# The last tile of a fused feed-forward kernel: each product evacuated from a PSUM tile of its own, the kept partial accumulated in PSUM, the last product in two column halves

## The chip, the cores and the metric

One core of a Trainium2 chip. The metric is the device time of one execution in microseconds (us).

Engines: PE does matmuls, DVE is VectorE, ACT is ScalarE, SP issues most transfers. PSUM is the memory that PE writes its results to. The kernel takes it in pieces of 512 FP32 values per partition, called banks here. To evacuate a result is to take it out of PSUM with another engine.

## The reference

```python
def reference(A_x, A_wqkv, A_wo, B_x, B_w_gate, B_w_up, B_w_down):
    xn = layernorm(A_x)                                  # 2048 x 1024, bf16
    s = linear_attention(xn, A_wqkv) @ A_wo              # 32 heads
    g = silu((silu(xn @ B_w_gate) * (xn @ B_w_up)) @ B_w_down)   # F = 3584
    return A_x + s * g
```

(Shortened: the linear attention is not touched by the change.)

## The kernel before

The down product `h @ w_down` is computed for a pass of 1024 tokens by 2x2 blocks, with seven block products in place of eight. A block here is 128 tokens by 512 output columns. A first phase leaves partial sums (`kept`: `s1` and the pair `s34`, FP32, in SBUF). A second phase adds three more products for each 128-token tile `t`, each a sum over `NFG` = 14 steps, each step one matmul: the pair `zw` and then `x_`. The last tile of the last pass is handled by `finish`, in which the products run one after the other so that the pair can be evacuated while the last product runs.

Shortened, with the pool lines simplified:

```python
CW = 512; NFG = 14; P = 128
pps = ctx.tile_pool(name="p3ps", bufs=4, space=PSUM)   # one bank each
ppd = ctx.tile_pool(name="p3pd", bufs=2, space=PSUM)   # two banks each
# ... (cut)
def fin(p, t, cc, y, eng1, eng2, out_eng, cols=None):  # y * s + x, then store
    # ... (cut: io holds x and s, loaded earlier)
    eng1.tensor_tensor(out=y[:, cs], in0=y[:, cs], in1=io[:, 1, cs], op=ALU.mult)
    eng2.tensor_tensor(out=io[:, 0, cs], in0=y[:, cs], in1=io[:, 0, cs], op=ALU.add)
    out_eng.dma_start(out=out2[...], in_=io[:, 0, cs])
# ... (cut)
def mm(out, lhs, rhs, first, lastk):
    nc.tensor.matmul(out, lhsT=lhs, rhs=rhs, start=first, stop=lastk, skip_group_check=True)

def finish(t):
    alloc(t, "b")
    x_, _, zw = bk[t]
    s1, s34 = kept[t]
    for q in (1, 2):
        for k in range(NFG):
            prods_b(t, k, True)[q]()           # into zw[:, 0, :], then zw[:, 1, :]
    d = m4.tile([P, 2, CW], FP32, name="dd", tag="m4")
    c11 = k2([P, CW], FP32, "c11")[:]
    g_ = k2([P, 2, CW], BF16, "g12")
    g11 = k2([P, CW], BF16, "g11")[:]
    nc.vector.tensor_tensor(out=d[:], in0=zw[:], in1=s34, op=ALU.add)
    nc.scalar.activation(out=g_[:], in_=d[:], func=ACT.Silu, scale=rch)
    fin(p, t + TPB, 0, g_[:, 0, :], *fin_e)
    fin(p, t, 1, g_[:, 1, :], *fin_e)
    for k in range(NFG):
        prods_b(t, k, True)[0]()               # into x_
    hs_ = [slice(i * CW // 2, (i + 1) * CW // 2) for i in range(2)]
    for cs in hs_:
        nc.vector.tensor_tensor(out=c11[:, cs], in0=x_[:, cs], in1=s1[:, cs], op=ALU.add)
        nc.scalar.activation(out=g11[:, cs], in_=c11[:, cs], func=ACT.Silu, scale=rch)
    for cs in hs_:
        fin(p, t, 0, g11, *fin_e, cols=cs)
```

In the listings of the profile, L882 and L883 are the two operations of `fin` (called output operations below), L910 is the matmul of `mm`, and L994, L995, L1002 and L1003 are the adds and Silus of `finish`.

## Time and profile before

| | before |
|---|---|
| time, first 3 runs | 767.11 us median (766.46 to 768.77) |
| span of the profiled run | 767.3 us |
| last matmul ends | 761.36 us |
| last VectorE instruction ends | 764.54 us |
| from there to the end of the span | 2.77 us |

From the page of the kernel before, first the span and the busy time of PE (us, share of the span, number of instructions), then the chain of work that ended last, as shares of the span by engine:

```profile
span 767.3 us, 10482 instructions
...
PE 754.1 (98%) x3717; PEld 349.6 (46%) x3717; DVE 551.5 (72%) x1076; ACT 345.8 (45%) x473; POOL 287.4 (37%) x413
...
PE 92%; DVE 4%; ACT 1%; DMA 1%; issue 1%; SPq 0%; ACTq 0%; DVEq 0%
```

PE is busy 98% and holds 92% of the chain. Work of other engines counts only where PE doesn't cover it, and at the end of the kernel that is everything after the last matmul. Timeline of PE at the end of the kernel before (start us, length us, engine, line, operation, number merged); the first line holds the last two matmuls of the tile before and the 28 of the pair:

```profile
751.70 6.64 PE L910 MATMUL dzw<-w_sb,hT 128*128 128x512 f16 x30
758.17 3.19 PE L910 MATMUL dx<-w_sb,hT 128*128 128x512 bf16 x14
```

Timeline of DVE, and below it of ACT, in the same stretch; brackets give the idle time before the instruction and what ended it:

```profile
757.05 0.43 DVE L883 TENSOR_TENSOR io<-g,io 128x512 bf16<-128x512 bf16 x1
758.38 1.23 DVE L994 TENSOR_TENSOR dd<-dzw,kept 128x1024 f32<-128x1024 f32 x1 [0.90 <-PE dzw L910]
760.82 0.42 DVE L882 TENSOR_TENSOR g<-g,io 128x512 bf16<-128x512 bf16 x1 [1.21 <-ACT g L995]
...
762.07 0.42 DVE L883 TENSOR_TENSOR io<-g,io 128x512 bf16<-128x512 bf16 x1
762.41 0.75 DVE L1002 TENSOR_TENSOR c<-dx,kept 128x256 f32<-128x256 f32 x2
763.40 0.29 DVE L882 TENSOR_TENSOR g<-g,io 128x256 bf16<-128x256 bf16 x1 [0.24 <-ACT g L1003]
...
764.25 0.29 DVE L883 TENSOR_TENSOR io<-g,io 128x256 bf16<-128x256 bf16 x1
```

```profile
759.63 1.15 ACT L995 ACTIVATE g<-dd,hsc 128x1024 bf16<-128x1024 f32 x1 [4.28 <-DVE dd L994]
762.86 0.91 ACT L1003 ACTIVATE g<-c,hsc 128x256 bf16<-128x256 f32 x2 [2.08 <-DVE c L1002]
```

Read them together. DVE waits 0.90 us for both products of the pair although the first was complete 3 us earlier, adds 1024 columns at once, and waits 1.21 us for one wide Silu. Its four output operations for the pair then run until 762.49. PE ended at 761.36, so the half adds of the last product (L1002) start 1.05 us late, held up by DVE's own order of work, not by PE. From the last matmul to the last DVE instruction it is 3.18 us.

### The profile page before, as it was taken

Reading aid. Unit: us, or ns where it says so; the run is one execution under the profiler, and the core shown is the slowest. Engines: PE = TensorE matmul, PEld = TensorE weight load, DVE = VectorE, ACT = ScalarE, POOL = GpSimd, SP = SyncE. Lnnn points to the kernel's source line nnn. Section 1 sums busy time; section 2 is a strip of 40 time slices with the busy share of each in tenths; the row PEclk is TensorE's granted clock in tenths of the full one; section 3 lists DMA queues with packets and bytes.
Section 4 is the critical chain, followed back from the end, with each engine's and each line's share of the span. In section 5 each row is a group of like instructions: output and inputs, shape, how many; then the busy total and the mean of one; then the engine's idle time right before and its main releaser. Section 6 shows DMA issues by size and latency. Waiting matters only on the chain.

```text
span 767.3 us, 10482 instructions
## 1 busy us (share of the span) xinstructions
PE 754.1 (98%) x3717; PEld 349.6 (46%) x3717; DVE 551.5 (72%) x1076; ACT 345.8 (45%) x473; POOL 287.4 (37%) x413
## 2 busy tenths in 40 slices
PE   7999999999999999999999999999999999999996
PEld 3544444444444444444444444444444444444443
DVE  6788557997666588878889885358676776787335
ACT  3545667788853566566447411132323223201111
POOL 0477499959685255858656000110000000200000
PEclk9999999999999999999999999999999999999999
DMA  9945868769889769898888227399654444530923
GB/s 308 352 95 114 229 221 274 248 222 259 237 304 262 256 228 312 283 333 298 308 309 290 89 81 262 113 356 334 229 185 167 165 169 175 187 114 23 296 73 117
DMA packets 105396, 170.29 MB, mean 222 GB/s; under 512 B 34688, under 2 KB 82176, under 8 KB 94720
## 3 DMA queue, kind: packets, MB, share of 16 engines
q1 hardware_dynamic: 94960, 121.00, 50.3%
q0 software_dynamic: 7936, 44.31, 15.0%
q10 hardware_dynamic: 2448, 4.33, 1.6%
q8 instruction: 29, 0.48, 0.3%
q14 instruction: 23, 0.19, 0.1%
HBM read 111.67 MB, written 50.59 MB: 211 GB/s over the span
## 4 chain that ended last, share of the span: by engine, by line
PE 92%; DVE 4%; ACT 1%; DMA 1%; issue 1%; SPq 0%; ACTq 0%; DVEq 0%
PE zw L725 25%; PE kv_ps L486 14%; PE dzw L910 13%; PE xb L725 12%; PE s_ps L659 7%; PE yb L725 6%; PE dx L910 6%; PE q_ps L170 4%; PE dy L910 3%; PE kvz L508 1%; DMA xp<-in_A_x_dram 1%; DVE o_blk L640 1%; PE nd_ps L632 1%; DVE pqT L141 1%; DVE pqT L153 0%
## 5 line engine op out<-in xcount | busy, mean ns | idle before, releaser
L725 PEld LDWEIGHTS <-w_sb 128*128 128x128 f16 (+1 forms) x1568 | 152.2, 98 | 184.3 <-issue 1.7
L725 PE MATMUL xb<-xnT,w_sb 128*128 128x512 bf16 x448 | 115.0, 379 | 1.1 <-ACT sg L800 1.1
L486 PE MATMUL kv_ps<-wkv_sb,xnT 128*128 128x512 bf16 x512 | 115.5, 383 | 0.4 <-DVE xnT L473 0.2
L725 PE MATMUL zw<-xnT,w_sb 128*128 128x512 bf16 x448 | 105.8, 379 | 0.0
L725 PE MATMUL zw<-S,w_sb 128*128 128x512 f16 x448 | 105.8, 379 | 0.0
L280 POOL TENSOR_TENSOR w_sb<-w_sb 128x512 f16<-128x512 bf16 x42 | 48.9, 1165 | 96.7 <-DVE w_sb L268 36.3
L247 ACT ACTIVATE w_sb<-w_sb 128x2048 bf16<-128x2048 bf16 x42 | 79.9, 1902 | 9.1 <-DMA w_sb<-in_B_w_up_dram 7.1
L910 PE MATMUL dx<-w_sb,hT 128*128 128x512 bf16 x224 | 82.8, 379 | 0.0
L486 PEld LDWEIGHTS <-xnT 128*128 128x128 bf16 x512 | 49.0, 98 | 57.2 <-issue 2.4
L910 PEld LDWEIGHTS <-hT 128*128 128x128 bf16 (+1 forms) x448 | 43.8, 98 | 52.9
L910 PE MATMUL dzw<-w_sb,hT 128*128 128x512 f16 (+1 forms) x224 | 64.4, 379 | 0.0
L170 PE MATMUL q_ps<-xnT,wq_sb 128*128 128x512 bf16 x256 | 58.2, 379 | 0.0
L753 DVE SCALAR_TENSOR_TENSOR s<-yb,rc_all,s 128x512 f32<-128x512 f32 x42 | 31.5, 749 | 37.0 <-ACT s L752 37.0
L659 PE MATMUL s_ps<-wo_sb,oT 128*128 128x512 bf16 x256 | 57.8, 379 | 0.0
L725 PE MATMUL yb<-S,w_sb 128*128 128x512 f16 x224 | 57.4, 379 | 0.0
L801 ACT ACTIVATE sg<-cg 128x1024 bf16<-128x1024 f32 x28 | 29.6, 1057 | 56.6 <-DVE cg L794 56.6
L794 DVE SCALAR_TENSOR_TENSOR cg<-zw,rc_all,s 128x1024 f32<-128x1024 f32 x28 | 35.9, 1283 | 25.4 <-PE zw L725 14.0
L850 POOL TENSOR_TENSOR hs<-hT 128x512 f16<-128x512 bf16 x2 | 2.5, 1258 | 132.6 <-ACT sg L801 132.6
L281 POOL TENSOR_TENSOR w_sb<-w_sb 128x512 f16<-128x512 bf16 x42 | 50.1, 1193 | 3.3
L283 POOL TENSOR_TENSOR w_sb<-w_sb 128x512 f16<-128x512 bf16 x42 | 50.8, 1210 | 0.0
L282 POOL TENSOR_TENSOR w_sb<-w_sb 128x512 f16<-128x512 bf16 x42 | 49.8, 1186 | 0.0
L884 POOL DMA_DIRECT2D out_dram<-io x16 | 8.7, 542 | 101.9 <-DVE io L883 101.6
(148 smaller groups left out, 1099.3 us busy)
## 6 DMA issues: line engine op xcount, KB each, us to landing
w_sb<-pk_g SPq DMA_DIRECT2D x27, 1024.0 KB, 6.0
pk_g<-w_sb POOLq DMA_DIRECT2D x14, 1024.0 KB, 5.4
pk_u<-w_sb POOLq DMA_DIRECT2D x14, 1024.0 KB, 6.4
w_sb<-wd SPq DMA_DIRECT2D x14, 1024.0 KB, 5.0
w_sb<-pk_u SPq DMA_DIRECT2D x14, 1024.0 KB, 4.9
w_sb<-wd SPq DMA_DIRECT2D x14, 768.0 KB, 5.8
w_sb<-in_B_w_gate_dram SPq DMA_DIRECT2D x14, 512.0 KB, 5.3
w_sb<-in_B_w_down_dram SPq DMA_DIRECT2D x28, 256.0 KB, 4.5
```

The source lines that it names most:

```text
L170: nc.tensor.matmul(q_ps[:], lhsT=wq_sb[:, dc, g * P:(g + 1) * P], rhs=xn_ap(dc, btok), start=(dc == 0), stop=(dc == DC - 1))
L247: nc.scalar.activation(out=junk, in_=raw_view(key, t), func=ACT.Square, accum_out=asum[:])
L280: nc.gpsimd.tensor_tensor(out=T1, in0=b12, in1=b11, op=ALU.subtract)
L281: nc.gpsimd.tensor_tensor(out=T2, in0=b22, in1=T1, op=ALU.subtract)
L282: nc.gpsimd.tensor_tensor(out=T3, in0=b22, in1=b12, op=ALU.subtract)
L283: nc.gpsimd.tensor_tensor(out=T4, in0=b21, in1=T2, op=ALU.subtract)
L486: mm = nc.tensor.matmul(kv_ps[:], lhsT=xn_ap(dc, tok), rhs=wkv_sb[:, dc, c * CW:(c + 1) * CW], start=(dc == 0), stop=(dc == DC - 1))
L659: mm = nc.tensor.matmul(s_ps[:], lhsT=oT[:, c, ttok], rhs=wo_sb[:, c, cc * CW:(cc + 1) * CW], start=(c == 0), stop=(c == G - 1))
L725: mm = nc.tensor.matmul(out, lhsT=lhs(k), rhs=rhs(k), start=(first and k == 0), stop=(k == HK - 1), skip_group_check=True)
L753: nc.vector.scalar_tensor_tensor(out=s2[:], in0=y_[:], scalar=rc, in1=s1[:], op0=ALU.mult, op1=ALU.add)
L794: nc.vector.scalar_tensor_tensor(out=d12, in0=zw[:], scalar=rc, in1=s2[:, None, :].to_broadcast([P, 2, TB]), op0=ALU.mult, op1=ALU.add)
L910: nc.tensor.matmul(out, lhsT=lhs, rhs=rhs, start=first, stop=lastk, skip_group_check=True)
```

## The change

The intent: let the two products of the pair be evacuated one by one, so that DVE is free when the last product ends; take the last add off DVE by copying `s1` into PSUM beforehand and accumulating on it; and finish one column half of the last product while PE computes the other.

"Own banks" stands for the first of these: a PSUM tile, an add and a Silu for each product of the pair. The name misleads in one point: the two products lay in different banks before too, `zw[:, 0, :]` and `zw[:, 1, :]` of a tile of two. What is new is that each is added and passed through Silu by itself.

The whole diff:

```diff
             def finish(t):
-                alloc(t, "b")
-                x_, _, zw = bk[t]
+                ps = [ppd.tile([P, 2, CW], FP32, name="dz", tag="d")[:, 0, :]]
+                ps += [pps.tile([P, CW], FP32, name="df%d" % i, tag="s")[:] for i in range(3)]
                 s1, s34 = kept[t]
-                for q in (1, 2):
+                t1, t2 = slice(t * P, (t + 1) * P), slice(TB + t * P, TB + (t + 1) * P)
+                hs_ = [slice(i * CW // 2, (i + 1) * CW // 2) for i in range(2)]
+                for i in range(2):
+                    nc.scalar.copy(out=ps[2 + i][:, 0:CW // 2], in_=s1[:, hs_[i]])
+                for q, (r0, cc) in enumerate(((t + TPB, 0), (t, 1))):
                     for k in range(NFG):
-                        prods_b(t, k, True)[q]()
-                d = m4.tile([P, 2, CW], FP32, name="dd", tag="m4")
-                c11 = k2([P, CW], FP32, "c11")[:]
-                g_ = k2([P, 2, CW], BF16, "g12")
+                        lhs = h[:, 2 * k, t2].bitcast(F16) if q else h[:, 2 * k + 1, t2]
+                        mm(ps[q], lhs, wb(k, 2 - q), k == 0, k == NFG - 1)
+                    d = k2([P, CW], FP32, "d%d" % q)[:]
+                    g_ = k2([P, CW], BF16, "g%d" % q)[:]
+                    nc.vector.tensor_tensor(out=d, in0=ps[q], in1=s34[:, q, :], op=ALU.add)
+                    nc.scalar.activation(out=g_, in_=d, func=ACT.Silu, scale=rch)
+                    if q == 0:
+                        f0 = (r0, cc, g_)
+                fin(p, *f0, *fin_e)
+                fin(p, r0, cc, g_, *fin_e)
                 g11 = k2([P, CW], BF16, "g11")[:]
-                nc.vector.tensor_tensor(out=d[:], in0=zw[:], in1=s34, op=ALU.add)
-                nc.scalar.activation(out=g_[:], in_=d[:], func=ACT.Silu, scale=rch)
-                fin(p, t + TPB, 0, g_[:, 0, :], *fin_e)
-                fin(p, t, 1, g_[:, 1, :], *fin_e)
-                for k in range(NFG):
-                    prods_b(t, k, True)[0]()
-                hs_ = [slice(i * CW // 2, (i + 1) * CW // 2) for i in range(2)]
-                for cs in hs_:
-                    nc.vector.tensor_tensor(out=c11[:, cs], in0=x_[:, cs], in1=s1[:, cs], op=ALU.add)
-                    nc.scalar.activation(out=g11[:, cs], in_=c11[:, cs], func=ACT.Silu, scale=rch)
-                for cs in hs_:
+                for i, cs in enumerate(hs_):
+                    o_ = ps[2 + i][:, 0:CW // 2]
+                    for k in range(NFG):
+                        mm(o_, h[:, 2 * k + 1, t1], wb(k, 0)[:, cs], False, k == NFG - 1)
+                    nc.scalar.activation(out=g11[:, cs], in_=o_, func=ACT.Silu, scale=rch)
                     fin(p, t, 0, g11, *fin_e, cols=cs)
```

## The prediction

> **What bounds the kernel.** TensorE. The page gives PE 98% of the 767.3 us span at 0.9+ granted clock, and the chain of waits is 92% PE. The change touches only `finish`, which handles the last token tile of the last down stage, so it can pay only where PE no longer covers the other engines: after the last matmul. The timeline of the end shows:
>
> - PE runs the three products of `finish` from about 752.1 us: 28 matmuls of the two-bank pair to 758.34, then 14 of the last product to 761.36 (pitch 0.216 us for 512 columns).
> - DVE, in order: outputs of the tile before until 757.48; idle 0.90 until the pair ends; the 1024-wide add 758.38–759.61 (1.23 us); idle 1.21 for the ScalarE Silu (1.15 us); four output operations 760.82–762.49. Only then, 1.05 us after PE ended, come the two half adds (762.41–763.2), Silu (0.5 us each), four half-wide output operations, last end 764.54.
> - From there to the end of span 2.76 us: the output DMA (1.6 us from issue to landing) and the closing drains.
>
> So 3.2 us lie between the last matmul and the last DVE instruction; the chain of waits there goes through the wide add, wide Silu, and DVE.
>
> **What the change does.** PE's columns are unchanged (14+14 half matmuls instead of 14 full ones in the last product: 14 more matmuls and weight loads). A half matmul has 256 columns; the groups with 129–132 columns run at about 80 ns each (10.1–10.3 us busy for 128), 512 columns at 216 ns, so I estimate 0.108–0.115 us for 256, weight load hidden. The Trainium skill, "TensorE: Matmul & The Clock Gate", section "Back-to-back issue gap", gives N/2.4+2.5 ns, 109 ns; the trace agrees at 512. So PE should end within 0.1 us of 761.36.
>
> Removed: the 1024-wide add and Silu, both half adds. Added: two 512-wide adds (0.68 each), two 512-wide Silus (0.71), two 256-wide ScalarE copies into PSUM (under 0.45 us each, estimate from 0.585 for 512), at about 755.4–756.2, long before the last product starts.
>
> Estimated new order: first add 757.5–758.2 (in the former 0.90 us gap; its product is complete at 755.3); second add 758.38–759.06; its Silu to 759.8; four output operations 759.1–760.9; first half complete at about 759.85, Silu to 760.3, two DVE operations to 761.5; second half complete 761.4, Silu to 761.9, two DVE operations to 762.5, DMA.
>
> The last DVE end moves from 764.54 to about 762.5: 2.0 us less, all on the critical path: 1.05 us of DVE queueing, 0.4 of half add, and one half's output work overlapped. The DMA tail should stay near 2.76.
>
> Accumulating on the copied data rests on the has_written bits left set by earlier full-bank products ("PSUM — Partial Sum Buffer", "The four PSUM rules": engine writes leave the bits alone, the matmul adds where they are set). No run here shows it yet; it costs no time.
>
> **Prediction:** 767.11 − 2.0 = 765.1 us, range 763.8 to 766.8. Chances: faster by over 2% 0.003, within 2% 0.99, slower 0.007.
>
> **What would show it.** Right: 28 matmuls of 256 columns in the last 3.1 us of PE; no DVE idle wait for the pair before the first add; DVE free when the second half ends; about 1.1 us from last matmul to last DVE end (3.2 before). Wrong: half matmuls at 0.13 us or more; PE waiting for the copies or for a bank; the output operations of the first two products still running at 761.4.
>
> **What would make it wrong.** A 256-column pitch set by the weight load (up to +1 us), a longer DMA tail, or run spread: the three runs before span 2.3 us, larger than the gain.

## The result, and the profile after

| | before | after |
|---|---|---|
| time, 4 runs each | 767.8 us median (766.46 to 768.77) | 764.17 us median (763.73 to 764.54) |
| ratio | | 0.9954 (95%: 0.9935 to 0.9972) |
| span of the profiled run | 767.3 | 762.5 |
| first matmul of `finish` starts | 752.13 | 749.32 |
| last matmul ends | 761.36 | 758.58 |
| last matmul end to last VectorE end | 3.18 | 1.16 |
| from there to the end of the span | 2.77 | 2.75 |

A ratio here is the mean time of one kernel's runs over that of the other's of the same rounds, so it isn't quite the ratio of the medians. Executions over 1.5% slower than the fastest of the same kernel are left out of the means. (752.13 is worked out: 28 matmuls, 0.216 us apart, ahead of the end of the pair.)

The measured 764.17 us lies within the range, but the difference of the medians, 3.6 us, is larger than the 2.0 predicted. The page of the changed kernel, the same three lines:

```profile
span 762.5 us, 10513 instructions
...
PE 752.3 (99%) x3731; PEld 350.5 (46%) x3731; DVE 551.0 (72%) x1075; ACT 346.6 (45%) x476; POOL 287.7 (38%) x413
...
PE 90%; DVE 5%; DMA 2%; POOL 1%; issue 1%; ACT 1%; SPq 0%; ACTq 0%; DVEq 0%
```

(The chain's larger share of DVE isn't the tail: over the first 30 us it runs mostly through DVE and POOL after the change, and through PE before.)

Timelines of the changed kernel's end: PE, then DVE, then ACT.

```profile
749.32 3.19 PE L910 MATMUL dz<-w_sb,hT 128*128 128x512 f16 x14
752.34 6.24 PE L910 MATMUL df<-w_sb,hT 128*128 128x512 bf16 x42
```

```profile
754.35 0.68 DVE L997 TENSOR_TENSOR d<-dz,kept 128x512 f32<-128x512 f32 x1
755.56 0.69 DVE L997 TENSOR_TENSOR d<-df,kept 128x512 f32<-128x512 f32 x1 [0.53 <-PE df L910]
756.17 0.41 DVE L882 TENSOR_TENSOR g<-g,io 128x512 bf16<-128x512 bf16 x1
...
757.56 0.42 DVE L883 TENSOR_TENSOR io<-g,io 128x512 bf16<-128x512 bf16 x1
757.90 0.28 DVE L882 TENSOR_TENSOR g<-g,io 128x256 bf16<-128x256 bf16 x1
...
759.12 0.29 DVE L882 TENSOR_TENSOR g<-g,io 128x256 bf16<-128x256 bf16 x1 [0.61 <-ACT g L1008]
759.45 0.29 DVE L883 TENSOR_TENSOR io<-g,io 128x256 bf16<-128x256 bf16 x1
```

```profile
752.44 0.66 ACT L990 COPY df<-kept 128x256 f32<-128x256 f32 x2
...
758.62 0.47 ACT L1008 ACTIVATE g<-df,hsc 128x256 bf16<-128x256 f32 x1 [1.06 <-PE df L910]
```

The two adds are apart, DVE has finished the pair and the first half when the last half comes, and it waits 0.61 us for ACT. After the last matmul only one Silu of 256 columns and two half-wide output operations are left: 1.16 us. The copies into PSUM were done 2.3 us before the last product's first matmul. PE is not slower: from the first matmul of `finish` to the last end it took 9.26 us (758.58 − 749.32), against 9.23 (761.36 − 752.13).

So 2.0 us of the 4.8 us between the two spans lie in the tail, as predicted, and 2.8 us (752.13 − 749.32) lie ahead of it, in instructions that the change doesn't touch. The same row in both profiles shows one place: the mean granted clock of PE (the third column from the end, PEclk) from 12.0 to 15.5 us, first of before, then of after, under the header of that table.

```profile
core 0: us, PE busy (x) PEld busy (x) DVE busy (x) ACT busy (x) POOL busy (x), PEclk, DMA share, GB/s
12.00:15.50 3.50, 3.50 (x14) 1.33 (x12) 2.89 (x10) 1.26 (x3) 0.00 (x0) 0.53 1.09 355
```

```profile
12.00:15.50 3.50, 3.50 (x18) 1.60 (x17) 3.12 (x14) 1.47 (x3) 0.00 (x0) 1.00 1.09 356
```

The kernel before ran PE at half clock there for one window of 3.41 us (12.22 to 15.63), after PE had waited for the second normalized tile. Second, PE's waits differ. From the table of waits of PE, before and then after (who waited for whom, us in total, times, longest):

```profile
PE tr_ps L470 <- DVE xn L443: 2.6, 2, 2.4
...
PE xb L725 <- ACT sg L800: 1.1, 1, 1.1
```

```profile
PE tr_ps L470 <- DVE xn L443: 2.0, 1, 2.0
```

The wait at L725, near 335 us in before, is absent after the change. In the profile of before that ACT instruction stood behind one that had waited 5.7 us for a weight transfer. In the chain of waits, the input transfer ahead of the second tile lands at 9.00 us before and at 8.10 after. That, the window and the wait at L725 make up most of the 2.8 us: at the first matmul of L508 (26.39 and 24.42), behind the window, the two profiles are already 1.97 us apart.

The question for the experiments: is this difference ahead of the tail chance, or does the change cause it?

### The profile page after: what moved, and what is told of

It reads as the page before. It is cut to its first block, busy times and chain, and to the rows that moved or that the text cites. A ratio compares the mean times of both kernels' runs of the same rounds, so it can differ in the third digit from the quotient of the medians.

```text
span 762.5 us, 10513 instructions
## 1 busy us (share of the span) xinstructions
PE 752.3 (99%) x3731; PEld 350.5 (46%) x3731; DVE 551.0 (72%) x1075; ACT 346.6 (45%) x476; POOL 287.7 (38%) x413
## 4 chain that ended last, share of the span: by engine, by line
PE 90%; DVE 5%; DMA 2%; POOL 1%; issue 1%; ACT 1%; SPq 0%; ACTq 0%; DVEq 0%
PE zw L725 25%; PE xb L725 13%; PE dzw L910 12%; PE kv_ps L486 11%; PE s_ps L659 7%; PE yb L725 6%; PE dx L910 6%; PE q_ps L170 4%; PE dy L910 3%; DMA xnT<-xn 1%; PE df L910 1%; PE kvz L508 1%; DMA xp<-in_A_x_dram 1%; DVE o_blk L640 1%; PE nd_ps L632 1%
## 5 line engine op out<-in xcount | busy, mean ns | idle before, releaser
L725 PEld LDWEIGHTS <-w_sb 128*128 128x128 f16 (+1 forms) x1568 | 152.2, 98 | 182.8
L725 PE MATMUL xb<-xnT,w_sb 128*128 128x512 bf16 x448 | 115.0, 379 | 0.0
L725 PE MATMUL zw<-S,w_sb 128*128 128x512 f16 x448 | 105.8, 379 | 0.0
L725 PE MATMUL zw<-xnT,w_sb 128*128 128x512 bf16 x448 | 105.8, 379 | 0.0
L910 PE MATMUL dx<-w_sb,hT 128*128 128x512 bf16 x210 | 79.6, 379 | 0.0
L910 PE MATMUL dzw<-w_sb,hT 128*128 128x512 f16 x196 | 58.3, 379 | 0.0
L725 PE MATMUL yb<-S,w_sb 128*128 128x512 f16 x224 | 57.4, 378 | 0.0
```

The lines of the kernel that those rows point to most:

```text
L725: mm = nc.tensor.matmul(out, lhsT=lhs(k), rhs=rhs(k), start=(first and k == 0), stop=(k == HK - 1), skip_group_check=True)
```

## The experiments

Theory N (noise): the change is worth 2.0 us, all in the tail; what differs ahead of it differs from run to run in either kernel. Theory U (upstream): the change somehow also speeds up the earlier part, by 1.5 us on average, for instance by where its instructions or buffers come to lie. The parts of the change were tried one by one as well. All runs gave correct results. "Tail" below means last matmul end to last DVE end; the remaining stretch to the end of the span was 2.74 to 2.77 us in every profile. Tails are worked out from the rounded times of the timelines and are uncertain by up to 0.02 us.

### e1: the kernel before against itself

Edit: none.

> The kernel before, unchanged, against itself. Theory N (noise upstream): the change saves 2.0 us in the tail and the other 1.6 us of the measured 3.6 us is chance in the part ahead of the tail, which has the same instructions in both kernels. Then this run's ratio is 1.000 with an interval that includes 1, its single runs spread over about 2 us, some with a granted clock of 0.997 and some with 1.0, the lower clock going with the longer span; and in its profile the stretch from the first matmul of the final pair of products to the end of the span is 15.2 us (15.17 in the first profile), whatever the span is. Theory U (systematic upstream effect of the change): the same null ratio, but nearly all runs of the kernel before show the half-clock stretch of about 3.4 us near the start or the stall of PE near 335 us.

Measured: 767.81 us median (767.34 to 769.86, 6 runs), the kernel before on the same chip 766.23 (765.66 to 769.44, 11 runs), ratio 1.0018 (0.9998 to 1.0038). Two medians of one and the same kernel are 1.6 us apart: as much as the surplus that Theory U is to explain. The profile has a span of 765.4 us with a tail of 3.19 us (3.18 in the first profile), and the last matmul ends at 759.39, 1.97 us earlier than in the first profile of the same kernel. The half-clock window is absent, as the same row of its table shows:

```profile
12.00:15.50 3.50, 3.50 (x18) 1.58 (x17) 3.02 (x16) 1.09 (x2) 0.00 (x0) 1.00 1.09 355
```

So neither the half-clock window nor the wait at L725 belongs to the kernel before as such. The granted clock of a run was a poorer sign than expected, since it also counts half-clock windows after the last matmul: among the 11 runs, the four at 0.996 or 0.997 took 767.5 to 769.4 us and six of the other seven 765.7 to 766.2, but in this kernel's own six runs 768.08 and 767.34 us had 0.999 and 0.998 while 767.44 had 0.996.

### e2: the changed kernel again

Edit: none to the changed kernel.

> The changed kernel again, on a chip where the kernel before runs in the same rounds. Theory N: ratio 0.9974 (2.0 us less), some runs with a clock of 0.997 as well; tail from the first matmul of the final products to the end 13.2 us. Theory U: ratio 0.9954 again (3.5 us less), clock 1.0 in all runs.

Measured: 765.18 us median (763.83 to 767.76, 6 runs), ratio 0.9978 (0.9958 to 0.9998), clocks 0.998 to 1.0. That is 1.7 us less by the ratio, close to the 2.0 of Theory N; 0.9954 lies outside the interval. The tail is 1.16 us again. And this profile does have the wait at L725, 1.0 us long, that was absent from the first profile of the changed kernel. One run reached 767.76 us, above many of the kernel before: the changed kernel spreads by 4 us too.

### e3: own banks for the pair, nothing else

Shortened:

```diff
-    nc.vector.tensor_tensor(out=d[:], in0=zw[:], in1=s34, op=ALU.add)      # 1024 wide
-    nc.scalar.activation(out=g_[:], in_=d[:], func=ACT.Silu, scale=rch)
+    # after each of the two products, q = 0, 1, each in its own bank zs[q]:
+    nc.vector.tensor_tensor(out=d, in0=zs[q], in1=s34[:, q, :], op=ALU.add)
+    nc.scalar.activation(out=g_, in_=d, func=ACT.Silu, scale=rch)
     # last product, half adds, Silus and output operations as in the kernel before
```

> Only the first part of the change: the two products of the old pair each with its own PSUM bank, add and Silu; the last product full-width, with the two half adds on VectorE. From the trace: outputs of the first two products are done at 760.9 instead of 762.5, so VectorE waits for PE (761.4), then add, Silu, two output operations, end 763.57 instead of 764.54. Theory N: tail 14.2 us, 1.0 us less than before, ratio 0.9987. Theory U: about 2.5 us less, ratio 0.9967, since the code differs here too.

Measured: 766.59 us median (764.8 to 769.39, 6 runs), ratio 0.9993 (0.9972 to 1.0015), which doesn't separate 0.9987 from 1. The profile does: the tail is 2.25 us, 0.93 less than before (expected 1.0). Timeline of DVE:

```profile
759.22 0.42 DVE L883 TENSOR_TENSOR io<-g,io 128x512 bf16<-128x512 bf16 x1
760.24 0.76 DVE L1007 TENSOR_TENSOR c<-dx,kept 128x256 f32<-128x256 f32 x2 [0.60 <-PE dx L910]
```

The last matmul ends at 760.19, and the last line of DVE's timeline is:

```profile
762.15 0.29 DVE L883 TENSOR_TENSOR io<-g,io 128x256 bf16<-128x256 bf16 x1
```

DVE now waits 0.60 us for PE ahead of the half adds, where before it came 1.05 us late. The table by windows of this profile shows the half-clock window again, in code that differs from before only at the end:

```profile
12.00:15.50 3.50, 3.50 (x11) 1.21 (x9) 3.16 (x12) 1.18 (x3) 0.00 (x0) 0.54 1.09 355
```

With it, 14.68 us pass from the second tile's transposes (L470) to the first matmul of L508, in this profile and in the first of before; without it 13.60 us, in e1, in e2 and in the first profile of the changed kernel. The window costs 1.08 us there in both kernels. The profiles of e7 and e8 below have it too (14.47 and 14.67 us); e8 is the changed kernel with another cut.

### e5, e6, e7: the other combinations

The edits, shortened:

```diff
 # e5: own banks + copy into PSUM, last product one of 512 columns
+    nc.scalar.copy(out=x_[:], in_=s1)
+    mm(x_[:], h[:, 2 * k + 1, t1], wb(k, 0), False, k == NFG - 1)
+    nc.scalar.activation(out=g11[:, cs], in_=x_[:, cs], func=ACT.Silu, scale=rch)   # each half
 # e6: own banks + two column halves, kept partial added on VectorE
+    mm(xs[i], h[:, 2 * k + 1, t1], wb(k, 0)[:, cs], k == 0, k == NFG - 1)
+    nc.vector.tensor_tensor(out=c11[:, cs], in0=xs[i], in1=s1[:, cs], op=ALU.add)
 # e7: copy into PSUM + two column halves as in the change, pair kept wide
+    nc.vector.tensor_tensor(out=d[:], in0=zw[:], in1=s34, op=ALU.add)
```

> Own banks for the first two products and the kept partial copied into PSUM, but the last product one of 512 columns, its Silu in two halves after it. One look: only the tail of the profile counts, since the earlier runs showed that the part ahead of it varies by some 2 us by chance. Last matmul end to last VectorE end: 3.18 us in the kernel before, 1.16 in the changed one. From their durations: Silu 0.47 twice, four half-wide output operations of 0.29 starting 0.5 after PE: 1.7 us. If the column split matters little, it would be 1.2.

Measured: tail 1.68 us, as expected. The last lines of PE and of DVE:

```profile
756.61 3.19 PE L910 MATMUL dx<-w_sb,hT 128*128 128x512 bf16 x14
761.19 0.29 DVE L883 TENSOR_TENSOR io<-g,io 128x256 bf16<-128x256 bf16 x1
```

> Own banks and the last product in two column halves, without the copy into PSUM: the kept partial is added on VectorE for each half. After the last matmul: half add 0.42, then the first half's two output operations while Silu of the second runs, then the second half's two: 1.7 us from last matmul to last VectorE end (1.16 with the copy). Here the copy into PSUM would be worth 0.55 us.

Measured: tail 1.65 us, near the 1.7 expected. The same two lines:

```profile
755.99 3.22 PE L910 MATMUL df<-w_sb,hT 128*128 128x256 bf16 x28
760.57 0.29 DVE L883 TENSOR_TENSOR io<-g,io 128x256 bf16<-128x256 bf16 x1
```

> The copy into PSUM and the two column halves, but the first two products still share one wide add and one wide Silu as in the kernel before. VectorE's output operations for the pair then run until 1.13 us after the last matmul, and the four half-wide ones follow: 2.4 us from last matmul to last VectorE end. If the queue on VectorE did not matter, it would be 1.2.

Measured: tail 2.16 us, 0.24 less than expected. The timeline of DVE shows the end of the pair's output operations, 1.10 us after the last matmul (759.61), and the first of the four half-wide ones directly behind:

```profile
760.29 0.42 DVE L883 TENSOR_TENSOR io<-g,io 128x512 bf16<-128x512 bf16 x1
760.63 0.29 DVE L882 TENSOR_TENSOR g<-g,io 128x256 bf16<-128x256 bf16 x1
...
761.48 0.29 DVE L883 TENSOR_TENSOR io<-g,io 128x256 bf16<-128x256 bf16 x1
```

The queue on DVE is as expected; the four operations started 0.21 to 0.32 us apart, some of them before the one ahead had ended, and ended 1.06 us after the pair's, where I had counted 1.27.

The three single looks took 766.12, 765.49 and 766.3 us beside 766.12 of the kernel before. Such single times can't rank them. The tails can:

| | tail, us |
|---|---|
| before (4 profiles: first, e1, e4, e9) | 3.18 to 3.19 |
| own banks (e3) | 2.25 |
| copy + halves, pair wide (e7) | 2.16 |
| own banks + copy (e5) | 1.68 |
| own banks + halves (e6) | 1.65 |
| all three, the change (3 profiles: first, e2, e10) | 1.16 |

Own banks give 0.93 us alone and 1.00 as the last part added (e7 to the change). The copy into PSUM gives 0.57 on top of own banks and 0.49 as the last part. The column halves give 0.60 and 0.52.

### e4, e9, e10: both kernels with the early gap filled

```diff
+        for k in range(8):
+            nc.tensor.matmul(wps[:], lhsT=warm[:, 0:P], rhs=warm[:], start=True, stop=True)
         emit_TR(1)
```

These dummy matmuls stand where PE waits for the second normalized tile, before the stretch in which the half-clock window was seen.

> The kernel before with 8 more dummy matmuls of 512 columns (1.7 us) in the PE gap near 9 to 11 us, where PE waits for the second normalized tile; nothing else changed. Theory N says the half-clock stretch follows this gap by chance: with the gap filled the granted clock is 1.0 in all runs, the runs spread less, and the median falls by as much as the stretch costs times how often it came, at most 1.7 us (ratio 0.998 to 1.000); the tail stays 15.2 us. If the stretch comes from something else, clocks of 0.997 stay.

Measured: 766.86 us median (766.14 to 767.77, 6 runs), ratio 0.9997 (0.998 to 1.0013), clocks 0.998 or 0.999. The spread is 1.6 us, against 3.8 of the kernel before on that chip; in the profile the clock from 12.0 to 15.5 us is 1.00. The median did not fall. The clocks of 0.998 remain, against the letter of the expectation of 1.0; a half-clock window after the last matmul is in the profiles of this kernel too.

> The kernel before with the 8 dummy matmuls in the early gap, again, to be compared with the next run of the same rounds. No half-clock stretch near 7 us in the profile and granted clocks of 0.998 or more in all runs; single runs within about 1.7 us of each other, as in the earlier run of this kernel (766.14 to 767.77).

Measured: 765.91 us median (765.78 to 767.23, 5 runs), clocks 0.998 to 1.0, tail 3.18 us, no half-clock window ahead of the tail. (Its place in the other profiles was 11.2 to 15.6 us, not near 7 us as the expectation has it.)

> The changed kernel with the same 8 dummy matmuls. With the half-clock stretch taken out of both, Theory N expects the mean of its runs 2.0 us under that of the run before this one (between 1.3 and 2.7), and 1.16 us from last matmul to last VectorE end. Theory U expects 3.5 us less.

Measured: 764.72 us median (763.56 to 766.08, 6 runs), clocks 0.999 or 1.0, tail 1.16 us. Means of the runs: 764.73 against 766.25 in e9, 1.5 us less, within the 1.3 to 2.7 of Theory N. Its own profile shows PE's last matmul later than in e9's (759.79 against 758.04), so a difference of nearly 2 us ahead of the tail occurs, in either direction, with the half-clock window kept out of both. Not all of the spread is that window; the waits for data at the start and at L725 vary too.

### e8, e11: the cut at 384 + 128 columns

```diff
-                hs_ = [slice(i * CW // 2, (i + 1) * CW // 2) for i in range(2)]
+                hs_ = [slice(0, 3 * CW // 4), slice(3 * CW // 4, CW)]
```

> The changed kernel with the last product cut at 384 + 128 columns instead of 256 + 256. After the last matmul less is left: about 0.9 us instead of 1.16. But groups of about 130 columns took 80 ns a matmul, not the 55 that the columns need, so the last product should take 3.4 us instead of 3.04 to 3.06. Net: from its first matmul to the last VectorE end about 0.1 us later than in the changed kernel (4.4 us there), so no gain.

Measured: tail 1.01 us (one run, 764.77 us), and no loss on PE. Timeline of PE in this profile, the second product and the last one merged:

```profile
752.98 6.24 PE L910 MATMUL df<-w_sb,hT 128*128 128x512 bf16 x42
```

The 42 matmuls take 6.24 us, exactly as with 256 + 256. Start to start in the trace, the 128-column matmuls are 56 ns apart, the 256-column ones 109, the 384-column ones 163. My 80 ns was a reading error: it divided the busy time of a group of eight (0.62 us) by eight, and that time contains the whole length of the last one, 0.22 us in the trace. Start to start, the groups of 129 and 132 columns are 55 to 62 ns apart too. The tail was 0.1 us longer than hoped because the first piece's output operations kept DVE until 759.84:

```profile
759.48 0.36 DVE L883 TENSOR_TENSOR io<-g,io 128x384 bf16<-128x384 bf16 x1
759.76 0.22 DVE L882 TENSOR_TENSOR g<-g,io 128x128 bf16<-128x128 bf16 x1
```

> The changed kernel cut at 384 + 128, timed. Its tail was 0.15 us shorter than that of the changed kernel in one look, since 128-column matmuls came every 56 ns. Against the kernel before: about 2.2 us less in the tail, ratio 0.9972; the single runs will spread by some 2 to 4 us from the part ahead of the tail, so that 0.15 us against the changed kernel cannot be seen in the times.

Measured: 765.02 us median (763.73 to 767.99, 6 runs), ratio 0.9984 (0.9963 to 1.0005), tail 1.03 us in its profile. In the tail this version beats the changed kernel (1.16) by 0.13 to 0.15 us and the kernel before (3.18) by 2.15 to 2.17; in times of whole runs it is not to be told from the changed kernel, as expected.

### What follows for the two theories

Theory U expected a ratio near 0.9954 in e2, a gap of 3.5 us between e9 and e10, and, in e3 too, a faster earlier part along with different code at the end. None of this came. Runs of the kernel before and of the changed kernel, from the first result and the timed comparisons taken together (different chips mixed), give means of 767.27 us (32 runs, standard deviation 1.3) and 764.92 us (10 runs, 1.2): 2.3 us apart, with an uncertainty of about 0.45 us (one standard error, from those deviations). This agrees with 2.0 from the tail. Without the first comparison, which raised the question, it is 1.8 us (28 and 6 runs, standard error 0.6). An effect of some tenths of a us ahead of the tail can't be excluded by these times.

One of the chance events can be traced further. All changes of clock within a trace lie whole multiples of 3.413 us apart. Cut the 13 traces along this grid, from the first change on: each of the 17 stretches in which PE was busy for 1.21 us or less was followed by half clock (13 of them at the end of the kernel), and none of the 2867 with 1.48 us or more. So the window came where the late second tile left PE busy for only 1.03 to 1.21 us of the stretch before; in the first profile of the changed kernel it was 1.48. With the gap filled (e4, e9, e10) it was 2.77 or more. This is read from kept traces; no run was made to test it. What stays open is why the second tile or a weight transfer comes later in one run than in another.

## Why the prediction was right

- What bounds the kernel: right. PE holds 90 to 92% of the chain in both profiles, and only the stretch after the last matmul changed.
- The sum, "2.0 us less, all on the critical path": right. The tail went from 3.18 to 1.16 us, 2.02 less, and the stretch behind it stayed at 2.75 to 2.77. The step of 1.05 us for DVE queueing is the own banks (0.93 to 1.00 in e3 and e7); the half add, put at 0.4, is the copy (0.49 to 0.57), and the overlap of one half's output work, the remaining 0.55, is the column halves (0.52 to 0.60).
- "DVE free when the second half ends; about 1.1 us from last matmul to last DVE end": right, 1.16.
- "PE should end within 0.1 us of 761.36": right in the sense that `finish` took PE 9.26 us against 9.23. Its reason was partly wrong: the estimate of 80 ns for some 130 columns was mis-read and is 55 to 62 ns. For 256 columns the trace has 109 ns, so the mistake cost nothing here; it would have ruled out the cut of e8.
- Accumulating on the copied data: the results are correct in every kernel with the copy, and PE didn't wait for it, nor for a bank.
- The time, 765.1 us: within the range, with 764.17 in the first comparison and 765.18 in e2. The first lies only 0.4 us above the range's lower end, and that it lies so low is chance, not a larger gain. The prediction's warning that run spread is larger than the gain was needed: the first comparison's 3.6 us holds 1.6 us that the change didn't cause. Its own words named three runs with 2.3 us of spread; with more runs both kernels spread by about 4 us.

## What to carry to other kernels

When PE covers everything else, look at what stands between its last matmul and the end, write down each engine's order of work there, and ask what an engine is still doing for earlier results when the last one comes: here half of a gain of 2.0 us came from emptying VectorE's queue, and the rest from shortening what the last result needs. A gain of 0.3% can be proven in the profile of the stretch that changed, where it repeated within about 0.01 us in every profile of both kernels, while the times of whole runs, with 4 us of spread, gave anything between 1.5 and 3.6 us for it by their means. And read the pace of matmuls from start to start, not from the busy time of short groups.

## What the Trainium skill lacked or had wrong

- "TensorE: Matmul & The Clock Gate", section "Back-to-back issue gap", gives about 81 ns per matmul at 128 columns and 131 ns at 512 as measured in sustained streams with weight loads. Here, each with its own weight load, 128 columns came every 56 ns, 256 every 109 and 512 every 216; the page's formula N/2.4 + 2.5 ns, which it calls the isolated gap, gives 56, 109 and 216. For these streams the formula fits and the two sustained figures don't.
- The same page, section "What's actually happening", says that the clock gate works in a free-running window of 3413 ns and knows only half and full clock. The trace agrees: one window of 3.41 us at 0.5 ahead of the last matmul in 4 of the 13 profiles (the first of before, e3, e7, e8). The page advises against fitting a model to a count of slow matmuls and puts the penalty of the ramp below 1% of a typical span. The 1.08 us here are 0.14% of the span, so this is no error, but they are over half of the gain that was to be measured.
- "PSUM — Partial Sum Buffer", in its closing table ("Summary: rules for kernel authors"), says that data put into PSUM by VectorE or ScalarE ahead of an accumulation must be 0. Its section "The four PSUM rules" is more exact: the matmul adds where an earlier matmul left the written bit set, overwrites where it is clear, and 0 is the only value that is safe either way. Nonzero partials copied by ScalarE into banks that earlier products had filled gave correct results in the changed kernel, e5, e7, e8, e10 and e11. No run tried a bank whose bits were clear.
- "ScalarE: Activation LUTs", section "Step-by-step: what each stage is for", speaks of PSUM as the faster destination for ScalarE. No run shows a destination alone; for the source, a 256-column Silu took 0.45 to 0.47 us from PSUM (e7, the changed kernel) and 0.49 to 0.51 us from SBUF (before, e6). No page has these figures by source.
- No page says how busy PE must be in such a window to keep its full clock. Here 1.21 us or less of 3.413 was always followed by half clock, and 1.48 us or more never (13 profiles).
